# Linear attention over 32 heads on one core: stores issued from the first output on, and the written-out orders of all engines rearranged

## The chip, the core and the metric

The kernel runs on one core of a Trainium2 chip. A core has a matrix engine (PE in the profile, with its weight loads as PEld), two engines for elementwise work (VectorE, DVE; ScalarE, ACT), GpSimd (POOL), and SyncE (SP), which here only issues DMA transfers. The metric is the device time of one execution in microseconds (us), and less is better.

## The reference

Inputs q, k and v have the shape 1 x 32 x 2048 x 128 in bf16: 32 heads, 2048 rows of 128 values. Per head, with phi(x) = (x + 1 where x > 0, else exp(x)) + 1e-6:

```python
kv  = einsum("bhsd,bhse->bhde", phi_k, v)     # 128 x 128 per head, a sum over all rows
z   = einsum("bhsd->bhd", phi_k)
num = einsum("bhqd,bhde->bhqe", phi_q, kv)
den = einsum("bhqd,bhd->bhq", phi_q, z)[..., None] + 1e-6
out = num / den
```

So each head needs all of its k and v before any of its outputs, and 2 MB of q, k, v and output move per head (0.5 MB each).

## The kernel before, in words

A head's 2048 rows lie on 128 partitions as 16 tiles of 128 columns. phi(x) is taken apart into min(exp(x), 1) + 1e-6 and max(x, 0), and both parts go through the matrix engine as two matmuls into one sum. All names below are keys of the program; a key is an operation, the head, a dot and a part.

- `ldq`, `ldk`, `ldv` (L324, SP): loads of a head, 512 KB each, into buffers that hold seven heads (`NI`). `st` (L418, SP): the store of a head's output from one of twelve output buffers (`NO`); head 31 is stored in three parts.
- `ek` (L336, ACT) takes exp(k); `em` (L339, DVE) does the min and the add. `rkd` (L342, DVE) and `rkp` (L346, POOL) take max(k, 0), half of the tiles each. `v1` (L350, POOL) copies v beside a column of ones.
- `T` (L368, PE) transposes q's 16 tiles into PSUM. `eq` (L372, ACT) takes exp of it, `emq` (L374, DVE) the min and add; `rqa` (L378, ACT) and `rqb` (L381, DVE) take max(q, 0), half each.
- `kv` (L357, PE) sums the 32 matmuls of a head, in two parts of 16; `kvs` (L362, ACT) copies the 128 x 129 result out of PSUM.
- `n` (L389, L394, L396, PE) makes numerators and denominators: `n.0` for 12 tiles in four PSUM banks, `n.1` for 4 tiles in two. `r` (L403, DVE) inverts the denominators, `f` (L410, DVE) multiplies. Constants (`ident`, `ones`, `eps0` to `eps2`, `v1ones`) are set up first, and `w0` to `w2` (L315) are warm-up matmuls.

Every engine runs its operations in the order written in the table `ORDER` (lines 83 to 144), strictly, and waits on counting semaphores for the dependencies that `add` is given. There is no loop that decides anything at run time. The dependencies that matter here: `T(h)` waits until `eq`, `rqa` and `rqb` of head h-1 have read PSUM; `n(h+1).0` waits until `f(h).0` has emptied the banks; `kvs(h)` waits for both parts of `kv(h)`; `st(h)` waits for both parts of `f(h)`; a load of head h waits until head h-7 has left its buffer. SP is one queue in order, so a store that waits holds back each load behind it.

Two waits of POOL are there by choice and not for data (`gate`, called with the head from the third on):

```python
return [f"r{h - 3}.0"] if name == "v1" else [f"f{h - 3}.0"]
```

So `v1(h)` may not start before `r(h-3).0` has ended, nor `rkp(h)` before `f(h-3).0`.

Of the kernel before, what the change touches and what calls it, by code (L numbers as in the profile page):

```python
# [74 lines left out]
def rqb_parts(h):  # L75
    if na(h) == 16:
        return ()
    if h == NH - 1:
# [3 lines left out]

ORDER = {
    "PE": """
        w2 w1 T0.0 T0.1 w0 kv0.0 kv0.1 T1.0 n0.0 kv1.0 kv1.1 n0.1 T2.0 n1.0 kv2.0 kv2.1 T3.0 n1.1 kv3.0 kv3.1 n2.0
        T4.0 n2.1 kv4.0 kv4.1 n3.0 T5.0 n3.1 kv5.0 kv5.1 n4.0 T6.0 n4.1 kv6.0 kv6.1 n5.0 T7.0 n5.1 kv7.0 kv7.1 n6.0
        T8.0 n6.1 kv8.0 kv8.1 n7.0 T9.0 n7.1 kv9.0 kv9.1 n8.0 T10.0 n8.1 kv10.0 kv10.1 n9.0 T11.0 n9.1 kv11.0 kv11.1
        n10.0 T12.0 n10.1 kv12.0 kv12.1 n11.0 T13.0 n11.1 kv13.0 kv13.1 n12.0 T14.0 n12.1 kv14.0 kv14.1 n13.0 T15.0
# [5 lines left out]
        n30.0 n30.1 n31.0 n31.1 n31.2  # L94
    """,
    "DVE": """
        rkd0.0 v1ones0 em0.0 eps0 em0.1 rkd1.0 rqb0.0 ones emq0.0 eps2 emq0.1 eps1 em1.0 v1ones1 r0.0 rqb1.0 f0.0
        rkd2.0 rkd3.0 emq1.0 em2.0 em3.0 r1.0 emq2.0 rqb2.0 r0.1 f0.1 rkd4.0 f1.0 em4.0 rqb3.0 r1.1 rkd5.0 f1.1 r2.0
        emq3.0 f2.0 em5.0 rqb4.0 r2.1 rkd6.0 f2.1 r3.0 emq4.0 f3.0 em6.0 rqb5.0 r3.1 rkd7.0 f3.1 r4.0 emq5.0 f4.0
        em7.0 rqb6.0 r4.1 rkd8.0 f4.1 r5.0 emq6.0 f5.0 em8.0 rqb7.0 r5.1 rkd9.0 f5.1 r6.0 emq7.0 f6.0 em9.0 rqb8.0  # L100
        r6.1 f6.1 emq8.0 r7.0 rkd10.0 f7.0 em10.0 rqb9.0 r7.1 f7.1 emq9.0 r8.0 rkd11.0 f8.0 em11.0 r8.1 rqb10.0 f8.1
        rkd12.0 r9.0 emq10.0 f9.0 em12.0 r9.1 rqb11.0 f9.1 rkd13.0 r10.0 emq11.0 f10.0 em13.0 r10.1 rqb12.0 f10.1
        emq12.0 r11.0 rkd14.0 f11.0 em14.0 r11.1 rqb13.0 f11.1 emq13.0 r12.0 rkd15.0 f12.0 em15.0 rqb14.0 r12.1
        rkd16.0 f12.1 r13.0 emq14.0 f13.0 em16.0 r13.1 rqb15.0 f13.1 rkd17.0 r14.0 emq15.0 f14.0 em17.0 rqb16.0
        r14.1 rkd18.0 f14.1 r15.0 emq16.0 f15.0 em18.0 rqb17.0 r15.1 rkd19.0 f15.1 r16.0 emq17.0 f16.0 em19.0
        rqb18.0 r16.1 rkd20.0 f16.1 r17.0 emq18.0 f17.0 em20.0 rqb19.0 r17.1 f17.1 emq19.0 r18.0 rkd21.0 f18.0
        em21.0 r18.1 rqb20.0 f18.1 emq20.0 r19.0 rkd22.0 f19.0 em22.0 r19.1 rqb21.0 f19.1 rkd23.0 r20.0 emq21.0
        f20.0 em23.0 r20.1 rqb22.0 f20.1 emq22.0 r21.0 rkd24.0 f21.0 em24.0 rqb23.0 r21.1 f21.1 rkd25.0 r22.0
        emq23.0 f22.0 em25.0 r22.1 rqb24.0 f22.1 emq24.0 r23.0 rkd26.0 f23.0 em26.0 rqb25.0 r23.1 rkd27.0 f23.1
        r24.0 emq25.0 f24.0 em27.0 r24.1 rqb26.0 f24.1 rkd28.0 r25.0 emq26.0 f25.0 em28.0 r25.1 rqb27.0 f25.1  # L110
        rkd29.0 r26.0 emq27.0 f26.0 em29.0 rqb28.0 r26.1 rkd30.0 f26.1 r27.0 emq28.0 f27.0 em30.0 r27.1 rqb29.0
        f27.1 rkd31.0 r28.0 emq29.0 f28.0 em31.0 r28.1 rqb30.0 f28.1 r29.0 emq30.0 f29.0 emq31.2 emq31.0 r29.1 f29.1
        r30.0 f30.0 r30.1 emq31.1 f30.1 r31.0 f31.0 r31.1 r31.2 f31.1 f31.2
    """,
    "ACT": """
        eq0.0 rqa0 ek0.0 ek0.1 eq0.1 ek1.0 kvs0 eq1.0 rqa1 ek2.0 kvs1 ek3.0 eq2.0 rqa2 kvs2 ek4.0 eq3.0 kvs3 rqa3
        ek5.0 eq4.0 kvs4 rqa4 ek6.0 eq5.0 kvs5 rqa5 ek7.0 eq6.0 kvs6 rqa6 ek8.0 eq7.0 kvs7 rqa7 ek9.0 eq8.0 kvs8
        rqa8 ek10.0 eq9.0 kvs9 rqa9 ek11.0 eq10.0 kvs10 rqa10 ek12.0 eq11.0 kvs11 rqa11 ek13.0 eq12.0 kvs12 rqa12
        ek14.0 eq13.0 kvs13 rqa13 ek15.0 eq14.0 kvs14 rqa14 ek16.0 eq15.0 kvs15 rqa15 ek17.0 eq16.0 kvs16 rqa16
        ek18.0 eq17.0 kvs17 rqa17 ek19.0 eq18.0 kvs18 rqa18 ek20.0 eq19.0 kvs19 rqa19 ek21.0 eq20.0 kvs20 rqa20  # L120
        ek22.0 eq21.0 kvs21 rqa21 ek23.0 eq22.0 kvs22 rqa22 ek24.0 eq23.0 kvs23 rqa23 ek25.0 eq24.0 kvs24 rqa24
        ek26.0 eq25.0 kvs25 rqa25 ek27.0 eq26.0 kvs26 rqa26 ek28.0 eq27.0 kvs27 rqa27 ek29.0 eq28.0 kvs28 rqa28
        ek30.0 eq29.0 kvs29 rqa29 ek31.0 eq30.0 kvs30 rqa30 eq31.2 eq31.0 eq31.1 kvs31 rqa31
    """,
    "POOL": """
        ident0 ident rkp0.0 v10.0 v10.1 v11.0 rkp1.0 rkp2.0 v12.0 rkp3.0 v13.0 v14.0 rkp4.0 v15.0 rkp5.0 v16.0
# [3 lines left out]
        v128.0 rkp28.0 v129.0 rkp29.0 v130.0 rkp30.0 v131.0 rkp31.0  # L130
    """,
    "SP": """
        ldq0.0 ldk0.0 ldv0.0 ldk1.0 ldq1.0 ldv1.0 ldk2.0 ldk3.0 ldq2.0 ldv2.0 ldq3.0 ldk4.0 ldv3.0 ldv4.0 ldk5.0
        ldq4.0 ldk6.0 ldv5.0 ldq5.0 ldk7.0 ldv6.0 ldv7.0 ldq6.0 ldk8.0 ldq7.0 ldv8.0 ldk9.0 ldq8.0 ldq9.0 ldv9.0
        st0.0 ldq10.0 ldv10.0 ldk10.0 ldk11.0 ldk12.0 ldk13.0 ldv11.0 ldv12.0 ldv13.0 ldq11.0 ldq12.0 ldv14.0 st1.0
        ldk14.0 ldk15.0 ldk16.0 ldq13.0 ldk17.0 ldv15.0 ldv16.0 ldq14.0 ldq15.0 ldv17.0 ldk18.0 ldq16.0 ldq17.0
        ldq18.0 st2.0 ldq19.0 ldk19.0 ldv18.0 ldk20.0 st3.0 st4.0 ldv19.0 ldk21.0 ldq20.0 st5.0 ldq21.0 st6.0 st7.0
        ldv20.0 st8.0 ldq22.0 ldv21.0 ldv22.0 ldk22.0 ldk23.0 ldv23.0 st9.0 ldq23.0 st10.0 ldk24.0 ldk25.0 ldq24.0
        ldv24.0 ldv25.0 ldv26.0 ldq25.0 ldq26.0 st11.0 ldv27.0 ldk26.0 st12.0 ldq27.0 ldk27.0 ldq28.0 st13.0 ldv28.0
        ldk28.0 st14.0 ldq29.0 ldk29.0 ldq30.0 ldv29.0 st15.0 ldv30.0 ldk30.0 st16.0 st17.0 ldk31.0 st18.0 st19.0  # L140
        ldv31.0 ldq31.0 st20.0 st21.0 st22.0 st23.0 st24.0 st25.0 st26.0 st27.0 st28.0 st29.0 st30.0 st31.0 st31.1
        st31.2
    """,
# [320 lines left out]
```

## Time and profile before

| | |
|---|---|
| median of four runs | 170.49 us (170.21 to 171.46) |
| the profiled execution: its time, and its span from the first to the last instruction | 171.01 us, 169.6 us |
| busy over the span: PE, DVE, ACT, POOL | 158.8, 154.6, 153.7, 85.2 us |
| DMA | 67.53 MB, mean 398 GB/s |
| granted clock of PE | 0.998 of full speed |

The page of the profile gives busy time for each engine, the span in 40 slices, the DMA queues, the chain of work that ended last, and groups of instructions by line. The trace behind it has every instruction with start and duration, and for each transfer the moments of issue and landing. Because each engine runs the written order, the n-th instruction of an engine is the n-th key of its list, and so every record can be given its key; the same holds for the transfers of SP. [...] the next instruction starts about 0.1 us before the end of the one ahead.

### The profile page before, as it was taken

What the parts mean: (1) busy time and instruction counts of PE and PEld (TensorE: products, weight loads), DVE (VectorE), ACT (ScalarE), POOL (GpSimd) and SP (SyncE); (2) the same over time, 40 slices, a digit from 0 to 9 for tenths busy, and PEclk for the clock granted to TensorE, in tenths of its full rate; (3) what the DMA queues carried; (4) which work ended last, traced back from release to release, by engine and by line L of the source; (5) the groups of instructions that cost most, each with busy time, mean ns of one, the idle gap of its engine ahead of it and who ended that gap; (6) DMA issues with size and microseconds to landing.
All of it is one profiled execution on the core that took longest, in us unless ns stands there. A gap on an engine that the chain in (4) does not pass through costs nothing.

```text
span 169.6 us, 6305 instructions
## 1 busy us (share of the span) xinstructions
PE 158.8 (94%) x2775; PEld 153.6 (91%) x2775; DVE 154.6 (91%) x267; ACT 153.7 (91%) x133; POOL 85.2 (50%) x71
## 2 busy tenths in 40 slices
PE   6988789999999999999999999999999999999950
PEld 2667689999999999999999999999999999999950
DVE  0189999999999999999999999999999999999893
ACT  3699959999999999999999999999999999997810
POOL 1436444566554555555555665456554566545000
PEclk9999999999999999999999999999999999999999
DMA  5999999999999999999999999999999999999875
GB/s 203 389 418 414 406 410 408 407 410 408 414 408 410 411 413 411 406 409 415 413 420 413 412 421 414 412 415 411 416 414 420 413 414 420 413 415 415 360 318 211
DMA packets 18748, 67.53 MB, mean 398 GB/s; under 512 B 2080, under 2 KB 2464, under 8 KB 18720
## 3 DMA queue, kind: packets, MB, share of 16 engines
q1 hardware_dynamic: 18720, 67.12, 98.5%
q8 instruction: 22, 0.36, 0.8%
q14 instruction: 6, 0.05, 0.1%
HBM read 50.33 MB, written 16.78 MB: 396 GB/s over the span
## 4 chain that ended last, share of the span: by engine, by line
PE 86%; DVE 8%; ACT 3%; issue 1%; POOL 0%; POOLq 0%
PE la L357 31%; PE la L394 19%; PE la L396 17%; PE la L368 16%; DVE la L410 3%; DVE la L374 2%; PE la L315 2%; DVE la L342 1%; ACT la L372 1%; ACT la L336 1%; DVE la L381 1%; PE la L389 1%; DVE la L403 1%; ACT la L378 1%; POOL la L301 0%
## 5 line engine op out<-in xcount | busy, mean ns | idle before, releaser
L410 DVE TENSOR_TENSOR la<-la 128x1536 bf16<-128x1536 f32 (+2 forms) x65 | 77.7, 1197 | 0.3
L396 PE MATMUL la<-la 128*128 128x129 bf16 x512 | 68.1, 220 | 0.0
L394 PE MATMUL la<-la 128*128 128x129 bf16 x512 | 68.1, 219 | 0.0
L372 ACT ACTIVATE la<-la 128x2048 bf16<-128x2048 bf16 (+2 forms) x35 | 60.4, 1731 | 5.2 <-PE la L368 3.5
L357 PE MATMUL la<-la 128*128 128x129 bf16 x1024 | 64.0, 219 | 0.3 <-DVE la L305 0.3
L336 ACT ACTIVATE la<-la 128x2048 bf16<-128x2048 bf16 (+1 forms) x33 | 61.3, 1861 | 0.0
L357 PEld LDWEIGHTS la<-la 128*128 128x128 bf16 x1024 | 60.0, 97 | 0.7 <-POOL la L350 0.7
L350 POOL COPY la<-la 128x1024 int32<-128x1024 int32 (+1 forms) x33 | 39.9, 1210 | 40.8 <-DVE la L403 30.7
L346 POOL TENSOR_SCALAR la<-la 128x1024 bf16<-128x1024 bf16 x32 | 44.7, 1397 | 29.2 <-DVE la L410 25.2
L396 PEld LDWEIGHTS la<-la 128*128 128x128 bf16 x512 | 49.5, 97 | 0.0
L394 PEld LDWEIGHTS la<-la 128*128 128x128 bf16 x512 | 47.1, 97 | 0.0
L389 PE MATMUL la<-la 128*128 128x3 bf16 (+1 forms) x192 | 32.3, 168 | 4.1 <-DVE la L410 1.5
L368 PE MATMUL la<-la 128*128 128x128 bf16 x512 | 33.9, 219 | 0.4 <-DVE la L381 0.4
L378 ACT ACTIVATE la<-la 128x1024 bf16<-128x1024 bf16 (+1 forms) x32 | 33.5, 1046 | 0.0
L368 PEld LDWEIGHTS la<-la 128*128 128x128 bf16 x512 | 29.4, 98 | 1.3 <-DVE la L381 0.6
L339 DVE TENSOR_SCALAR la<-la 128x2048 bf16<-128x2048 bf16 (+1 forms) x33 | 23.0, 699 | 2.8 <-ACT la L336 2.8
L389 PEld LDWEIGHTS la<-la 128*128 128x128 bf16 x192 | 18.7, 97 | 4.9 <-DVE la L410 1.7
L374 DVE TENSOR_SCALAR la<-la 128x2048 bf16<-128x2048 bf16 (+2 forms) x35 | 22.7, 650 | 0.2
L381 DVE TENSOR_SCALAR la<-la 128x1024 bf16<-128x1024 bf16 x31 | 20.9, 674 | 0.8 <-ACT la L372 0.3
L342 DVE TENSOR_SCALAR la<-la 128x1024 bf16<-128x1024 bf16 x32 | 15.1, 475 | 5.5 <-DMA la<-in_k_dram 5.5
L403 DVE RECIPROCAL la<-la 128x12 f32<-128x12 f32 (+2 forms) x65 | 13.0, 201 | 2.7 <-PE la L396 1.0
L362 ACT ACTIVATE la<-la 128x129 bf16<-128x129 f32 x32 | 9.0, 282 | 1.9 <-PE la L357 1.9
(14 smaller groups left out, 11.7 us busy)
## 6 DMA issues: line engine op xcount, KB each, us to landing
la<-in_q_dram SPq DMA_DIRECT2D x32, 512.0 KB, 15.3
la<-in_k_dram SPq DMA_DIRECT2D x32, 512.0 KB, 14.9
la<-in_v_dram SPq DMA_DIRECT2D x32, 512.0 KB, 15.4
out_dram<-la SPq DMA_DIRECT2D x31, 512.0 KB, 15.3
out_dram<-la SPq DMA_DIRECT2D x2, 192.0 KB, 2.5
out_dram<-la SPq DMA_DIRECT2D x1, 128.0 KB, 2.7
```

Of the source, the lines that this page charges most:

```text
L336: add("ACT", f"ek{h}.{i}", lambda e, a=a, b=b: e.activation(em_sb[:, h % NE, a:b], k_sb[:, h % NI, a:b], ACT.Exp), over("ldk", h, ld_parts ...
L346: add("POOL", f"rkp{h}.{i}", lambda e, a=a, b=b: e.tensor_scalar(rk_sb[:, h % NR, a:b], k_sb[:, h % NI, a:b], BIG, 0.0, op0=ALU.min, op1=A ...
L350: add("POOL", f"v1{h}.{i}", lambda e, a=a, b=b: e.tensor_copy(v1_sb[:, h % NV, a:b, 0:D].bitcast(i32), v_sb[:, h % NI, a:b].bitcast(i32)), ...
L357: ins = e.matmul(kv_ps, lhsT=src[:, j], rhs=v1_sb[:, h % NV, j, 0:NC], start=(j + part == 0), stop=(j == NT - 1 and part == 1))
L368: ins = e.transpose(xT[:, j], q_sb[:, h % NI, j], ident[:])
L372: add("ACT", f"eq{h}.{i}", lambda e, a=a, b=b: e.activation(emq_sb[:, h % NQ, a:b], xT[:, a:b], ACT.Exp), over("T", h, t_parts, a, b) + fr ...
L374: add("DVE", f"emq{h}.{i}", lambda e, a=a, b=b: e.tensor_scalar(emq_sb[:, h % NQ, a:b], emq_sb[:, h % NQ, a:b], 1.0, EPS, op0=ALU.min, op1 ...
L378: add("ACT", f"rqa{h}", lambda e: e.activation(rq_sb[:, h % NQ, 0:n], xT[:, 0:n], ACT.Relu), over("T", h, t_parts, 0, n) + freed(NQ, h, (" ...
L389: e.matmul(_ap(o_ps[:, :], o + D, [[NC, m]]), lhsT=ones[:], rhs=epsr[:, 0:m], start=True, stop=False, skip_group_check=True)
L394: e.matmul(to, lhsT=emq_sb[:, h % NQ, t], rhs=kvs_sb[:, h % NK], start=False, stop=False, skip_group_check=True)
L396: ins = e.matmul(to, lhsT=rq_sb[:, h % NQ, t], rhs=kvs_sb[:, h % NK], start=False, stop=True, skip_group_check=True)
L410: return e.tensor_tensor(out=_ap(o_sb[:, :, :, :], first(o_sb[:, h % NO, t0, 0:1]) - first(o_sb[:, :, :, :]), [[m * D, nb], [D, m], [1, D] ...
```

## The change

Only the table `ORDER` is changed. No operation, size, buffer or dependency differs. On SP the first stores move ahead among the loads (`st0` from place 31 to place 18, `st1` from 44 to 34, and then about one store for four loads), so that the stores are spread over the loads; from `ldv31` on the list is as before. PE swaps two warm-ups and `n0.1` with `T2.0`. ACT takes both parts of `eq0` first and moves `eq31.2`. DVE's list is rearranged at the start and end and in the places of `rkd` and `rqb` among its neighbours in the middle.

```diff
 ORDER = {
     "PE": """
-        w2 w1 T0.0 T0.1 w0 kv0.0 kv0.1 T1.0 n0.0 kv1.0 kv1.1 n0.1 T2.0 n1.0 kv2.0 kv2.1 T3.0 n1.1 kv3.0 kv3.1 n2.0
+        w1 w2 T0.0 T0.1 w0 kv0.0 kv0.1 T1.0 n0.0 kv1.0 kv1.1 T2.0 n0.1 n1.0 kv2.0 kv2.1 T3.0 n1.1 kv3.0 kv3.1 n2.0
...
     "DVE": """
-        rkd0.0 v1ones0 em0.0 eps0 em0.1 rkd1.0 rqb0.0 ones emq0.0 eps2 emq0.1 eps1 em1.0 v1ones1 r0.0 rqb1.0 f0.0
-        rkd2.0 rkd3.0 emq1.0 em2.0 em3.0 r1.0 emq2.0 rqb2.0 r0.1 f0.1 rkd4.0 f1.0 em4.0 rqb3.0 r1.1 rkd5.0 f1.1 r2.0
+        eps0 rkd0.0 v1ones0 em0.0 rqb0.0 em0.1 v1ones1 eps2 emq0.0 rkd1.0 ones emq0.1 eps1 em1.0 r0.0 rqb1.0 f0.0
+        emq1.0 rkd2.0 em2.0 rkd3.0 r1.0 em3.0 rqb2.0 emq2.0 r0.1 f0.1 rkd4.0 f1.0 em4.0 rqb3.0 r1.1 rkd5.0 f1.1 r2.0
...
         r6.1 f6.1 emq8.0 r7.0 rkd10.0 f7.0 em10.0 rqb9.0 r7.1 f7.1 emq9.0 r8.0 rkd11.0 f8.0 em11.0 r8.1 rqb10.0 f8.1
-        rkd12.0 r9.0 emq10.0 f9.0 em12.0 r9.1 rqb11.0 f9.1 rkd13.0 r10.0 emq11.0 f10.0 em13.0 r10.1 rqb12.0 f10.1
-        emq12.0 r11.0 rkd14.0 f11.0 em14.0 r11.1 rqb13.0 f11.1 emq13.0 r12.0 rkd15.0 f12.0 em15.0 rqb14.0 r12.1
+        r9.0 rkd12.0 emq10.0 f9.0 em12.0 r9.1 rqb11.0 f9.1 rkd13.0 r10.0 emq11.0 f10.0 em13.0 r10.1 rqb12.0 f10.1
+        rkd14.0 r11.0 emq12.0 f11.0 em14.0 rqb13.0 r11.1 rkd15.0 f11.1 r12.0 emq13.0 f12.0 em15.0 rqb14.0 r12.1
...
-        rqb18.0 r16.1 rkd20.0 f16.1 r17.0 emq18.0 f17.0 em20.0 rqb19.0 r17.1 f17.1 emq19.0 r18.0 rkd21.0 f18.0
+        rqb18.0 r16.1 f16.1 r17.0 rkd20.0 emq18.0 f17.0 em20.0 rqb19.0 r17.1 f17.1 rkd21.0 r18.0 emq19.0 f18.0
...
-        f20.0 em23.0 r20.1 rqb22.0 f20.1 emq22.0 r21.0 rkd24.0 f21.0 em24.0 rqb23.0 r21.1 f21.1 rkd25.0 r22.0
-        emq23.0 f22.0 em25.0 r22.1 rqb24.0 f22.1 emq24.0 r23.0 rkd26.0 f23.0 em26.0 rqb25.0 r23.1 rkd27.0 f23.1
-        r24.0 emq25.0 f24.0 em27.0 r24.1 rqb26.0 f24.1 rkd28.0 r25.0 emq26.0 f25.0 em28.0 r25.1 rqb27.0 f25.1
-        rkd29.0 r26.0 emq27.0 f26.0 em29.0 rqb28.0 r26.1 rkd30.0 f26.1 r27.0 emq28.0 f27.0 em30.0 r27.1 rqb29.0
-        f27.1 rkd31.0 r28.0 emq29.0 f28.0 em31.0 r28.1 rqb30.0 f28.1 r29.0 emq30.0 f29.0 emq31.2 emq31.0 r29.1 f29.1
-        r30.0 f30.0 r30.1 emq31.1 f30.1 r31.0 f31.0 r31.1 r31.2 f31.1 f31.2
+        f20.0 em23.0 rqb22.0 r20.1 rkd24.0 f20.1 r21.0 emq22.0 f21.0 em24.0 rqb23.0 r21.1 f21.1 r22.0 rkd25.0
+        emq23.0 f22.0 em25.0 rqb24.0 r22.1 f22.1 emq24.0 r23.0 rkd26.0 f23.0 em26.0 rqb25.0 r23.1 rkd27.0 f23.1
+        r24.0 emq25.0 f24.0 em27.0 r24.1 rqb26.0 f24.1 rkd28.0 r25.0 emq26.0 f25.0 em28.0 r25.1 rqb27.0 f25.1 r26.0
+        rkd29.0 emq27.0 f26.0 em29.0 rqb28.0 r26.1 f26.1 rkd30.0 r27.0 emq28.0 f27.0 em30.0 rqb29.0 r27.1 rkd31.0
+        f27.1 r28.0 emq29.0 f28.0 em31.0 r28.1 rqb30.0 f28.1 r29.0 emq30.0 f29.0 emq31.0 emq31.1 r29.1 f29.1 r30.0
+        f30.0 r30.1 emq31.2 f30.1 r31.0 f31.0 r31.1 r31.2 f31.1 f31.2
     """,
     "ACT": """
-        eq0.0 rqa0 ek0.0 ek0.1 eq0.1 ek1.0 kvs0 eq1.0 rqa1 ek2.0 kvs1 ek3.0 eq2.0 rqa2 kvs2 ek4.0 eq3.0 kvs3 rqa3
+        eq0.0 eq0.1 ek0.0 ek0.1 rqa0 ek1.0 kvs0 eq1.0 rqa1 ek2.0 kvs1 ek3.0 eq2.0 rqa2 kvs2 ek4.0 eq3.0 kvs3 rqa3
...
-        ek30.0 eq29.0 kvs29 rqa29 ek31.0 eq30.0 kvs30 rqa30 eq31.2 eq31.0 eq31.1 kvs31 rqa31
+        ek30.0 eq29.0 kvs29 rqa29 ek31.0 eq30.0 kvs30 rqa30 eq31.0 eq31.1 kvs31 eq31.2 rqa31
...
     "SP": """
-        ldq0.0 ldk0.0 ldv0.0 ldk1.0 ldq1.0 ldv1.0 ldk2.0 ldk3.0 ldq2.0 ldv2.0 ldq3.0 ldk4.0 ldv3.0 ldv4.0 ldk5.0
-        ldq4.0 ldk6.0 ldv5.0 ldq5.0 ldk7.0 ldv6.0 ldv7.0 ldq6.0 ldk8.0 ldq7.0 ldv8.0 ldk9.0 ldq8.0 ldq9.0 ldv9.0
-        st0.0 ldq10.0 ldv10.0 ldk10.0 ldk11.0 ldk12.0 ldk13.0 ldv11.0 ldv12.0 ldv13.0 ldq11.0 ldq12.0 ldv14.0 st1.0
...
-        ldk28.0 st14.0 ldq29.0 ldk29.0 ldq30.0 ldv29.0 st15.0 ldv30.0 ldk30.0 st16.0 st17.0 ldk31.0 st18.0 st19.0
+        ldq0.0 ldk0.0 ldv0.0 ldk1.0 ldq1.0 ldv1.0 ldk2.0 ldq2.0 ldk3.0 ldv2.0 ldq3.0 ldk4.0 ldv3.0 ldv4.0 ldk5.0
+        ldq4.0 ldv5.0 st0.0 ldk6.0 ldq5.0 ldv6.0 ldv7.0 ldk7.0 ldq6.0 ldq7.0 ldq8.0 ldk8.0 ldv8.0 ldv9.0 ldk9.0
+        ldq9.0 ldk10.0 ldq10.0 st1.0 ldk11.0 ldq11.0 ldv10.0 st2.0 ldq12.0 ldv11.0 ldk12.0 ldq13.0 st3.0 ldv12.0
+        ldk13.0 ldv13.0 st4.0 ldv14.0 ldk14.0 ldv15.0 st5.0 ldq14.0 ldk15.0 ldq15.0 ldk16.0 ldk17.0 st6.0 ldv16.0
+        ldv17.0 ldk18.0 ldq16.0 ldv18.0 ldq17.0 ldq18.0 ldv19.0 st7.0 ldk19.0 ldk20.0 ldk21.0 st8.0 ldq19.0 ldk22.0
+        ldq20.0 ldv20.0 st9.0 ldq21.0 ldv21.0 ldv22.0 st10.0 ldq22.0 ldk23.0 st11.0 ldq23.0 ldk24.0 ldv23.0 st12.0
+        ldq24.0 ldk25.0 ldv24.0 st13.0 ldq25.0 ldk26.0 ldv25.0 ldv26.0 st14.0 ldq26.0 ldk27.0 st15.0 ldv27.0 ldq27.0
+        ldk28.0 st16.0 ldv28.0 ldk29.0 ldq28.0 st17.0 ldv29.0 ldq29.0 ldk30.0 ldv30.0 st18.0 ldk31.0 ldq30.0 st19.0
         ldv31.0 ldq31.0 st20.0 st21.0 st22.0 st23.0 st24.0 st25.0 st26.0 st27.0 st28.0 st29.0 st30.0 st31.0 st31.1
         st31.2
```

More of the change, by code (lines that the diff above doesn't have):

```diff
@@ L101 @@
         r6.1 f6.1 emq8.0 r7.0 rkd10.0 f7.0 em10.0 rqb9.0 r7.1 f7.1 emq9.0 r8.0 rkd11.0 f8.0 em11.0 r8.1 rqb10.0 f8.1
-        rkd12.0 r9.0 emq10.0 f9.0 em12.0 r9.1 rqb11.0 f9.1 rkd13.0 r10.0 emq11.0 f10.0 em13.0 r10.1 rqb12.0 f10.1
-        emq12.0 r11.0 rkd14.0 f11.0 em14.0 r11.1 rqb13.0 f11.1 emq13.0 r12.0 rkd15.0 f12.0 em15.0 rqb14.0 r12.1
-        rkd16.0 f12.1 r13.0 emq14.0 f13.0 em16.0 r13.1 rqb15.0 f13.1 rkd17.0 r14.0 emq15.0 f14.0 em17.0 rqb16.0
+        r9.0 rkd12.0 emq10.0 f9.0 em12.0 r9.1 rqb11.0 f9.1 rkd13.0 r10.0 emq11.0 f10.0 em13.0 r10.1 rqb12.0 f10.1
@@ L105 @@
+        rkd14.0 r11.0 emq12.0 f11.0 em14.0 rqb13.0 r11.1 rkd15.0 f11.1 r12.0 emq13.0 f12.0 em15.0 rqb14.0 r12.1
+        rkd16.0 f12.1 r13.0 emq14.0 f13.0 em16.0 rqb15.0 r13.1 rkd17.0 f13.1 r14.0 emq15.0 f14.0 em17.0 rqb16.0
         r14.1 rkd18.0 f14.1 r15.0 emq16.0 f15.0 em18.0 rqb17.0 r15.1 rkd19.0 f15.1 r16.0 emq17.0 f16.0 em19.0
-        rqb18.0 r16.1 rkd20.0 f16.1 r17.0 emq18.0 f17.0 em20.0 rqb19.0 r17.1 f17.1 emq19.0 r18.0 rkd21.0 f18.0
-        em21.0 r18.1 rqb20.0 f18.1 emq20.0 r19.0 rkd22.0 f19.0 em22.0 r19.1 rqb21.0 f19.1 rkd23.0 r20.0 emq21.0
@@ L113 @@
-        r30.0 f30.0 r30.1 emq31.1 f30.1 r31.0 f31.0 r31.1 r31.2 f31.1 f31.2
+        rqb18.0 r16.1 f16.1 r17.0 rkd20.0 emq18.0 f17.0 em20.0 rqb19.0 r17.1 f17.1 rkd21.0 r18.0 emq19.0 f18.0
+        em21.0 r18.1 rqb20.0 f18.1 rkd22.0 r19.0 emq20.0 f19.0 em22.0 r19.1 rqb21.0 f19.1 rkd23.0 r20.0 emq21.0
+        f20.0 em23.0 rqb22.0 r20.1 rkd24.0 f20.1 r21.0 emq22.0 f21.0 em24.0 rqb23.0 r21.1 f21.1 r22.0 rkd25.0
+        emq23.0 f22.0 em25.0 rqb24.0 r22.1 f22.1 emq24.0 r23.0 rkd26.0 f23.0 em26.0 rqb25.0 r23.1 rkd27.0 f23.1
@@ L132 @@
     "SP": """
-        ldq0.0 ldk0.0 ldv0.0 ldk1.0 ldq1.0 ldv1.0 ldk2.0 ldk3.0 ldq2.0 ldv2.0 ldq3.0 ldk4.0 ldv3.0 ldv4.0 ldk5.0
-        ldq4.0 ldk6.0 ldv5.0 ldq5.0 ldk7.0 ldv6.0 ldv7.0 ldq6.0 ldk8.0 ldq7.0 ldv8.0 ldk9.0 ldq8.0 ldq9.0 ldv9.0
-        st0.0 ldq10.0 ldv10.0 ldk10.0 ldk11.0 ldk12.0 ldk13.0 ldv11.0 ldv12.0 ldv13.0 ldq11.0 ldq12.0 ldv14.0 st1.0
[L136 to L139, printed above, removed]
-        ldk28.0 st14.0 ldq29.0 ldk29.0 ldq30.0 ldv29.0 st15.0 ldv30.0 ldk30.0 st16.0 st17.0 ldk31.0 st18.0 st19.0
+        ldq0.0 ldk0.0 ldv0.0 ldk1.0 ldq1.0 ldv1.0 ldk2.0 ldq2.0 ldk3.0 ldv2.0 ldq3.0 ldk4.0 ldv3.0 ldv4.0 ldk5.0
[6 more added lines that the diff above has]
+        ldk28.0 st16.0 ldv28.0 ldk29.0 ldq28.0 st17.0 ldv29.0 ldq29.0 ldk30.0 ldv30.0 st18.0 ldk31.0 ldq30.0 st19.0
         ldv31.0 ldq31.0 st20.0 st21.0 st22.0 st23.0 st24.0 st25.0 st26.0 st27.0 st28.0 st29.0 st30.0 st31.0 st31.1
```

## The prediction

> **What bounds the kernel now.** I read the page first, for who is full and where in the span.
>
> ```profile
> span 169.6 us, 6305 instructions
> PE   6988789999999999999999999999999999999950
> DVE  0189999999999999999999999999999999999893
> ACT  3699959999999999999999999999999999997810
> DMA  5999999999999999999999999999999999999875
> ```
>
> A slice is 4.24 us. PE, DVE, ACT and DMA are all full from the sixth slice on; only the first 25 us and the last 9 us have room. In the trace `kv3.0` begins at 25.12 and `kv31.0` at 157.42, so 28 heads take 132.3 us, 4.725 us each, and every single head takes that: PE sets the pace there and waits for nothing. So the middle can only be kept or spoilt, and a gain must come from the start.
>
> Second, the waits, for what PE lacks at the start:
>
> ```profile
> ACT la L362 <- PE la L357: 1.9, 1, 1.9
> PE la L389 <- DVE la L374: 1.2, 1, 1.2
> PE la L389 <- DVE la L306: 0.8, 1, 0.8
> PE la L389 <- ACT la L362: 0.6, 1, 0.6
> ```
>
> `n0.0` waited 0.8 us for the constant `eps1`, `n1.0` 1.2 us for `emq1.0`. The timeline of DVE and of POOL around that wait shows why `emq1.0` was late:
>
> ```profile
> 15.28 1.74 DVE L410 TENSOR_TENSOR la<-la 128x1536 bf16<-128x1536 f32 x1
> 16.93 2.19 DVE L342 TENSOR_SCALAR la<-la 128x1024 bf16<-128x1024 bf16 x2
> 19.05 0.68 DVE L374 TENSOR_SCALAR la<-la 128x2048 bf16<-128x2048 bf16 x1
> ...
> 16.63 1.04 POOL L350 COPY la<-la 128x1024 int32<-128x1024 int32 x1 [1.47 <-DMA la<-in_v_dram]
> 17.64 1.21 POOL L346 TENSOR_SCALAR la<-la 128x1024 bf16<-128x1024 bf16 x1
> ```
>
> Two `rkd` (L342, two instructions in one row) took 2.19 us ahead of `emq1.0` (L374), where one takes 0.42 us alone. Each ended 0.28 us after a POOL instruction ended (17.67 and 18.85): they stood still meanwhile.
>
> Third, the end. `f31.2` ends at 166.83 and the last store lands at 169.55, 2.72 us later. By the landing marks the transfers before it land 1.2 to 1.28 us apart, but for four steps of 2.2 to 2.8 that I take as they are, until `st30` at 167.64, so DMA is no more than about a microsecond behind PE as a bound.
>
> **What the Trainium skill says.** "SBUF — State Buffer", section "SBUF: two separate sides": VectorE in its two-port modes and GpSimd share a pair of ports as an exclusive lock, held for a whole instruction, and the loser "fully blocks". The trace agrees (rows above). It shows more: with one instruction waiting on each side they alternate. `rkp3` waited for `rkd2` and then went ahead of `rkd3`; `rkp1` for `emq0.1`, and ahead of `em1.0`. After the lock is won, POOL needs 0.89 us more and a full-head DVE instruction 0.55. "VectorE: DVE Perf Modes", section "Why PSUM operands drop a tier", explains why `rqb` and `f`, which read PSUM, ran beside POOL unslowed (0.69 and 1.75 us with and without): they don't use both ports.
>
> **The change, part by part.**
>
> *Start.* I rewrote the start with the new orders, the old durations and the lock. ACT: `eq0.1` ahead of `ek0` and `rqa0` behind it leaves `ek1.0` at 10.15 (was 10.17) and `kvs0` at 11.95, nothing. `eps1` is now ahead of `em1.0`, so `n0.0` starts when `kvs0` ends, 12.3 for 12.91: gain 0.6. `T2.0`, no longer behind `n0.1`, starts when `kv1` is through, 15.6 (was 17.52). `f0.0` ends at 16.45; `emq1.0` comes next, starts at 16.36, ahead of `v12`, whose data land at 16.58, and ends at 17.0. `n0.1` still waits for `kvs1` (17.0), then `n1.0` follows at 17.5 instead of 19.78. Now `rkd2`, `em2.0` and POOL's `v12`, `rkp3` alternate: 17.89, 18.17, 19.06, and `em2.0` ends at 19.6, so `kv2` starts at 19.65 (was 21.27): 1.6. `T3.0` waits for `rqa2` (21.4) and `rqb2` (21.3): 21.5 for 23.71. `emq2.0` at 21.25 is 0.4 us ahead of `v13`. `f0.1` ends at 22.65 (was 24.53), `f1.0` at 24.7. `kv3` starts after `n1.1` at 23.2 (was 25.12), `n2.0` at 25.0 (26.96), `T4.0` at 26.8 once `rqa3` is done (28.45). Gain at head 4: **1.65 us**. Loads for it: `ldq4` lands at 25.26 and `ldk5` at 23.97, in time. If either race of `emq` against `v1` (margins of 0.4 us) is lost, about 0.7 us of it goes.
>
> *Stores.* Landing by place in the queue doesn't change: 1.266 us after a load for a load, 1.281 load to store, 1.207 store to load, 1.241 store to store (means of the trace); the new mixture has four more of each turn, and sums to 0.08 us less over the whole queue. `st0` at place 18 makes SP wait for `f0.1`. The 17 loads ahead of it last until 26.5, and a transfer takes 2.4 us beyond its data time (`st31.2`: 2.7 for 128 KB), so DMA runs dry only if `f0.1` ends after 24.1; 22.65 is early enough. Cost 0; with the old 24.53 it would be 0.4. Further stores follow their `f` by 19 us or more: no wait. Loads become later against their users, since stores go ahead of them: the closest are `ldq30` with 1.1 us (was 11), `ldk30` 1.1, `ldq16` 1.4. So loads cover a shift of about 1.1 us, not more.
>
> *Middle.* In heads 9, 17, 22 and 26 `rkd` moves from ahead of `r.0` to behind it: `r rkd emq f`. DVE does the same work, but `r(h)` releases `v1(h+3)`. Head 9 before:
>
> ```profile
> 61.89 0.42 DVE L342 TENSOR_SCALAR la<-la 128x1024 bf16<-128x1024 bf16 x1
> 62.22 0.23 DVE L403 RECIPROCAL la<-la 128x12 f32<-128x12 f32 x1
> 62.36 0.63 DVE L374 TENSOR_SCALAR la<-la 128x2048 bf16<-128x2048 bf16 x1
> 62.91 1.75 DVE L410 TENSOR_TENSOR la<-la 128x1536 bf16<-128x1536 f32 x1
> ...
> 62.51 1.37 POOL L350 COPY la<-la 128x1024 int32<-128x1024 int32 x1 [1.18 <-DVE la L403]
> ```
>
> Before, `emq10` had the lock when `v112` came. Now `rkd12` has it, `v112` waits, and by the alternation goes ahead of `emq10`. `r9.0` starts 0.33 earlier, but behind it come `rkd12`, 0.89 of copy and then `emq10`: `f9.0` ends 0.85 us later (the copy less what rounding leaves), against a slack of 0.10 between `f9.0` and `n10.0`. The bounds are 0 (POOL doesn't go first) and 0.85; I take **0.75 us**, kept to the end because PE has no slack. In heads 17, 22 and 26 the copy's data land at 99.9, 123.8 and 142.8 by place. With PE 0.9 us early, `emq` is under way before that, and costs nothing.
>
> *End.* The new places of `eq31` and `emq31` move work before 160.9, where `r30.0` waits for PE; then the same chain runs from `n30.0`. 0.
>
> *Sum.* PE: -1.65 + 0.75 = -0.9, so `f31.2` ends at 165.9 and its store could land at 168.65. DMA: `st30` lands at 167.56, and `st31`'s 512 KB need 1.25 us at the queue's pace, 168.8, or 168.5 at the pace in which its parts landed before. I take 168.7 for the span of 169.55 to the last landing: -0.85. The profiled execution would go from 171.01 to 170.16; the median, which stands 0.52 lower, from 170.49 to **169.6 us**.
>
> **Rivals.**
> 1. *Races lost at the start.* `v12` or `v13` takes the lock first: -0.9 at the start, +0.75 at head 9: 170.3. For it: margins of 0.4 us; against: landings at the start are even.
> 2. *Slower: the lock is lost in all four heads.* If PE isn't at least about 0.1 us early on reaching head 17, `v120`'s data are there when `rkd20` runs, the 0.75 is paid, and then at 22 and 26 too. With a start that gains only 0.6: -0.6 + 4 x 0.75 = +2.4, 172.9; with 1.0, half that. Against: the start must miss by a microsecond. It decides from a start gain below 0.7 us.
> 3. *SP's wait at `st0` leaves DMA dry*, with `f0.1` as late as before: the DMA end moves by 0.4, to 170.05.
> 4. *No lock at head 9*: PE is 1.1 us early, where loads stop it, and DMA still ends at 168.7: 169.6 as well.
>
> **How the numbers follow.** About 0.5%, 0.85 us, is what a measurement of this kernel can tell from no change. Forecast with rival 4: 0.53 (169.2 to 170.0, somewhat over half of it beyond the bound); rivals 1 and 3: 0.24 (170.0 to 170.9); rival 2: 0.18 (171.3 to 172.9); a gain past the DMA end, by a better pace of the mixture: 0.05. Faster: 0.31 + 0.05 = 0.36. Slower: 0.18 and 0.06 of unforeseen delays within rival 1: 0.24. Same: 0.40. Range 169.0 to 171.8, which leaves out most of rival 2 and little below.
>
> **What would show it.** `n1.0` at about 17.5 and `T4.0` near 26.8; SP idle at `st0` until about 22.7 with DMA still full; an `emq10` of some 1.5 us with PE idle before `n10.0`, and no such at 17, 22, 26; heads of 4.725 us elsewhere; `f31.2` near 165.9 with DMA full beyond it. Wrong if PE shows waits for loads after head 10, if more than one `emq` is stretched, or if `T4.0` is later than 28.

## The result, and the profile after

The changed kernel is slower: 171.41 us median of 35 runs (170.09 to 172.60) against 170.87 us of 54 runs of the kernel before (170.02 to 171.46). The ratio is **1.0036, with a 95% interval of 1.0024 to 1.0048**. Its runs spread over 2.5 us, those of before over 1.4. A ratio, here and below, leaves out runs more than 1.5% above the fastest of the same kernel, which matters in experiment 7 alone. The profiled execution took 170.84 us, the fourth fastest of the 35. Its span is 169.4 us, where the median span of the 35 runs is 170.1 and the profile of before has 169.6. So this page shows where PE and DMA gained and lost time, but not the loss of the median run; for that the experiments are needed.

The page of the changed kernel, its head and the rows in 40 slices:

```profile
span 169.4 us, 6304 instructions
PE   6988989999999999999999999999999999999950
DVE  0187999999999999999999999999999999999892
ACT  3799999999999999999999999999999999996800
DMA  5999999999999999999999999999999999999985
```

At this grain little differs but the start: ACT's sixth slice, half empty before (5), is full. There the forecast held closely. The timeline of DVE in the changed kernel (start, duration, operation) has `f0.0`, `emq1.0`, `rkd2.0`, `em2.0` in the new order, with `emq1.0` at 16.36 and no wait for the lock:

```profile
14.70 1.75 DVE L410 TENSOR_TENSOR la<-la 128x1536 bf16<-128x1536 f32 x1
16.36 0.68 DVE L374 TENSOR_SCALAR la<-la 128x2048 bf16<-128x2048 bf16 x1
16.96 0.42 DVE L342 TENSOR_SCALAR la<-la 128x1024 bf16<-128x1024 bf16 x1
17.30 0.69 DVE L339 TENSOR_SCALAR la<-la 128x2048 bf16<-128x2048 bf16 x1
```

`n1.0` starts at 17.51, `kv3.0` at 23.22, `f0.1` ends at 22.64, `T4.0` starts at 26.55 (28.45 before): PE is **1.90 us early** from head 3 on. At the end it is 0.69 us early (`f31.2` 166.14, before 166.83). The last store still lands at 169.40, 3.26 us after `f31.2`, because `st30` landed at 168.07, later than before (167.64). So two things need a cause: 1.2 us of PE's lead is lost on the way, and DMA, which now sets the end, isn't earlier than before but 0.4 us later.

**Where PE's lead goes.** The waits of POOL for v, first of the kernel before, then of the changed one (total, times, longest):

```profile
POOL la L350 <- DMA la<-in_v_dram: 9.2, 5, 2.7
```

```profile
POOL la L350 <- DMA la<-in_v_dram: 27.2, 13, 3.1
```

Ten of the thirteen are copies from head 10 on that start when their data land, after their gate; in the kernel before only `v131` does. What that does is seen in the timeline of the changed kernel around head 8, DVE and then POOL:

```profile
51.46 1.75 DVE L410 TENSOR_TENSOR la<-la 128x1536 bf16<-128x1536 f32 x1
53.12 1.38 DVE L339 TENSOR_SCALAR la<-la 128x2048 bf16<-128x2048 bf16 x1
...
52.92 1.04 POOL L350 COPY la<-la 128x1024 int32<-128x1024 int32 x1 [3.08 <-DMA la<-in_v_dram]
```

The gate would have placed `v110` under `f7.0` (51.46 to 53.21), which reads PSUM. Its data came at 52.80, so it took the port pair 0.2 us ahead of `em10.0` (L339), which then took 1.38 us where 0.68 is usual. PE's lead falls there from 1.91 to 1.38. `em23`, `em24` and `em25` (0.93, 0.95, 0.99 us) take 0.7 more together, for the same reason. No `emq` is stretched, at head 9 either: the data of `v112` landed at 61.57, when `emq10` (60.79 to 61.48) was through.

**Where DMA's time goes.** SP has issued 17 loads by 10.7 us and then waits for `f0.1` until 22.67. The windows of the profile show what DMA does then. Each row has the stretch, its length, the busy time of PE, PEld, DVE, ACT and POOL, the clock, the busy share of DMA and its GB/s. The kernel before, and then the changed one:

```profile
23.00:26.00 3.00, 2.56 (x47) 2.38 (x45) 2.97 (x6) 2.70 (x3) 1.04 (x1) 1.00 1.03 408
26.00:29.00 3.00, 3.00 (x58) 2.99 (x56) 2.83 (x7) 3.00 (x4) 1.41 (x1) 1.00 1.02 407
```

```profile
23.00:26.00 3.00, 3.00 (x59) 3.00 (x57) 2.87 (x4) 2.97 (x4) 2.16 (x2) 1.00 1.00 377
26.00:29.00 3.00, 3.00 (x58) 2.99 (x56) 3.00 (x7) 3.00 (x3) 1.54 (x2) 1.00 0.99 392
```

(408 - 377) x 3 + (407 - 392) x 3 = 138 KB that DMA did not move, 0.34 us at its pace, in an execution in which `f0.1` was as early as forecast. A second profile of the changed kernel misses 183 KB.

### The profile page after: what moved, and what is told of

Read it like the earlier page. It is cut to its first block, busy times and chain, and to the rows that moved or that the text cites. A ratio compares the mean times of both kernels' runs of the same rounds, so it can differ in the third digit from the quotient of the medians.

```text
span 169.4 us, 6304 instructions
## 1 busy us (share of the span) xinstructions
PE 159.3 (94%) x2775; PEld 153.4 (91%) x2775; DVE 154.1 (91%) x267; ACT 154.3 (91%) x133; POOL 84.4 (50%) x71
## 4 chain that ended last, share of the span: by engine, by line
DVE 40%; ACT 30%; PE 24%; issue 3%; POOL 0%; DVEq 0%; POOLq 0%
DVE la L410 19%; ACT la L372 14%; ACT la L336 10%; PE la L357 8%; DVE la L381 6%; PE la L394 5%; ACT la L378 5%; DVE la L374 5%; PE la L368 5%; PE la L396 5%; DVE la L339 4%; DVE la L342 3%; DVE la L403 2%; PE la L315 2%; ACT la L362 1%
## 5 line engine op out<-in xcount | busy, mean ns | idle before, releaser
L339 DVE TENSOR_SCALAR la<-la 128x2048 bf16<-128x2048 bf16 (+1 forms) x33 | 24.5, 742 | 2.9 <-ACT la L336 2.9
L374 DVE TENSOR_SCALAR la<-la 128x2048 bf16<-128x2048 bf16 (+2 forms) x35 | 21.1, 603 | 0.0
```

The costliest lines, as they stand in the source:

```text
L339: add("DVE", f"em{h}.{i}", lambda e, a=a, b=b: e.tensor_scalar(em_sb[:, h % NE, a:b], em_sb[:, h % NE, a:b], 1.0, EPS, op0=ALU.min, op1=AL ...
```

## The experiments

Each ran beside the kernel before on the same chip, with a ratio to it. The three kinds of change (start, stores, middle of DVE) are taken apart first, then `st0` alone. The diffs of experiments 1, 3 and 10 are against the kernel before, those of 2, 5 and 7 against the changed one; "..." is what is left out of a long list. Two theories stand in the expectations from the start: A, late loads put `v1` on `em`; B, DMA is slower by itself when stores are mixed in early.

**1. The stores alone.**

```diff
     "SP": """
-        ... ldq4.0 ldk6.0 ldv5.0 ldq5.0 ...
+        ... ldq4.0 ldv5.0 st0.0 ldk6.0 ldq5.0 ...
```

> The kernel before with SP's new order alone (stores early), PE, DVE, ACT as before. Theory A (late loads: v1 copies that wait for their data fall on em, the port pair is taken, PE loses up to 0.5 us each time, and PE's head start of 1.9 us is what makes loads late): PE has no head start here, v1 is at most 0.1 us late at its gate, no em is stretched; ratio 0.999 to 1.001, at most 0.3 us for SP's wait at st0 (f0.1 ends at 24.5 here). Theory B (DMA itself is slower with stores mixed in from the start): the loss is all here, ratio 1.003 to 1.005, and the landing of st30 in the trace moves later by 0.5 us or more.

Measured 1.0068 (1.0042 to 1.0095), 172.40 us. Theory A missed, and B seemed nearer, with more than its 1.005; neither named the cause. `f0.1` ends at 24.6 here, and DMA moves 251 GB/s from 23 to 26 us and 328 from 26 to 29: 708 KB missing. `ldq31` lands at 156.00 (before 153.86), and late copies stretch `em20` and `em31` to 1.38 and 1.36 us.

**2. The engines alone**: the changed kernel with SP as before.

```diff
     "SP": """
-        ... ldq4.0 ldv5.0 st0.0 ldk6.0 ldq5.0 ...
+        ... ldq4.0 ldk6.0 ldv5.0 ldq5.0 ...
```

> The kernel after with SP's order of before: loads early, all other orders new. Theory A: PE is 1.9 us early at head 4 and no v1 is late for its data; but where rkd stands between r.0 and emq (heads 9, 17, 22, 26) the copy v1 is there and takes the port pair between the two, 0.75 us each; with two to four of these PE keeps 0 to 0.4 us: ratio 0.998 to 1.006. If the copy doesn't go ahead, PE keeps about 1.1 us and DMA's end bounds the kernel: ratio 0.995. Theory B: DMA as in the kernel before, ratio 0.995 to 1.000.

Measured 1.0086 (1.0058 to 1.0114), 172.82 us, the worst of the parts. The timeline of DVE and POOL at head 9 has the prediction's lock: `r9.0`, `rkd12`, `emq10`, `f9.0`, and `v112`:

```profile
60.73 0.22 DVE L403 RECIPROCAL la<-la 128x12 f32<-128x12 f32 x1
60.87 0.36 DVE L342 TENSOR_SCALAR la<-la 128x1024 bf16<-128x1024 bf16 x1
61.15 1.52 DVE L374 TENSOR_SCALAR la<-la 128x2048 bf16<-128x2048 bf16 x1
62.59 1.74 DVE L410 TENSOR_TENSOR la<-la 128x1536 bf16<-128x1536 f32 x1
...
61.01 1.11 POOL L350 COPY la<-la 128x1024 int32<-128x1024 int32 x1 [0.84 <-DVE la L403]
```

`emq10`, `emq18`, `emq23` and `emq27` each take 1.52 us for 0.63; PE loses 0.80, 0.74, 0.75 and 0.79 there and goes from 1.16 early to 1.89 late. With loads in time each of the four places costs what I had priced for one.

**3. The start alone**: the first lines of PE, DVE and ACT new (DVE's two as in the change), all else as before.

```diff
     "PE": """
-        w2 w1 T0.0 T0.1 ... kv1.1 n0.1 T2.0 n1.0 ...
+        w1 w2 T0.0 T0.1 ... kv1.1 T2.0 n0.1 n1.0 ...
     "ACT": """
-        eq0.0 rqa0 ek0.0 ek0.1 eq0.1 ek1.0 ...
+        eq0.0 eq0.1 ek0.0 ek0.1 rqa0 ek1.0 ...
```

> The kernel before with only the first lines of the orders of PE, DVE and ACT new (to head 5), stores and middle as before. Both theories: PE is 1.9 us early at head 4, no stretched em in the middle, loads stop PE at ldk28 to ldk30 so that about 1.1 us is kept; DMA ends at about 168.7 in the trace; ratio 0.994 to 0.997, a version faster than both. If the ratio is 0.999 or more, PE's lead is worth nothing because DMA alone sets the end.

Measured **0.9977** (0.9963 to 0.9991), 170.41 us: faster than both kernels. The size missed. PE is only 0.66 us early in this profile: `em2` and `emq2` lost the lock to `rkp3` and `v13` (1.53 and 1.56 us), the lost race of my first rival. Over all ten profiles with the new start PE's lead at head 4 is 0.66 to 2.04 us. No load stopped it.

**4. The changed kernel again.**

> The changed kernel once more, for a second profile and a ratio on the same chip: 1.0036 by its first measurement. Theory A: in a profile with a span near 170.1 more em instructions are stretched than the four of the first profile (em10, em23, em24, em25), and f31.2 ends near 167 or later. Theory B: f31.2 near 166.2 again and the landing of st30 later than 168.1.

Measured 1.0030 (1.0011 to 1.0050). The profiled span is 169.4 again, so what was expected of a longer one was not tried. Behind the start four `em` are stretched (`em10`, `em20`, `em25`, `em31`), and `f31.2` ends at 166.32.

**5. Start and stores, the middle of DVE as before.** One of the places in the list:

```diff
     "DVE": """
-        r9.0 rkd12.0 emq10.0 f9.0 ...
+        rkd12.0 r9.0 emq10.0 f9.0 ...
```

> The first lines of PE, DVE and ACT new and SP's order new, the middle of DVE as before: the changed kernel without its four heads of r, rkd, emq. Theory A (late loads put v1 on em): as the changed kernel, em10 and two to four of em20 to em31 stretched to 0.9 to 1.4 us, ratio 1.000 to 1.004, against 0.9977 of the same kernel with the stores as before. Theory B (the mixture of stores and loads makes DMA itself slower): the same ratio, but no difference in it from stretched em; st30 lands after 168.1. A third, that the new middle of DVE is the loss: 0.998.

Measured 1.0040 (1.0016 to 1.0064). As A has it, six `em` are stretched (0.79 to 1.16 us), and as B has it, `st30` lands at 168.62: the two are not told apart. It rules out the third: the middle of DVE isn't needed for the loss.

**6. The same with the loads sorted by due time**, stores in their places.

> As start_and_stores, each store at the same place, but the loads between them (from place 19 to 114) sorted by when they are due, a v by its gate. By place v25, v24, v23, v20 and v10, which were late by 0.7 to 1.8 us for a PE that is 1.9 us early, come in time; v28, v29 and v30 stay 0.9 to 1.9 us late. Theory A: no em stretched before em28, PE ends about as in start_only (f31.2 near 166.2), ratio 0.996 to 0.999. Theory B: no better than start_and_stores, 1.000 to 1.004.

Measured 1.0039 (1.0025 to 1.0053), no better, though no `em` before `em29` is stretched in the profile. So A, as stated, fell. (My sorting had its own price: `T29` waited 1.1 us for `ldq29`. But `st30` lands at 169.17, so DMA sets the end here too.) What experiments 1, 5 and 6 share is `st0` at place 18.

**7. `st0` alone moved later in the changed kernel.**

```diff
-        ldq4.0 ldv5.0 st0.0 ldk6.0 ldq5.0 ldv6.0 ldv7.0 ldk7.0 ldq6.0 ldq7.0 ...
+        ldq4.0 ldv5.0 ldk6.0 ldq5.0 ldv6.0 ldv7.0 ldk7.0 ldq6.0 st0.0 ldq7.0 ...
```

> The changed kernel with st0 alone moved from place 18 to 24. If part of the loss is the dip of DMA at 25.25 us behind SP's wait for f0.1, DMA gains up to 0.3 us and ldk6 to ldq6 land 1.25 us earlier: ratio 1.000 to 1.002. If st0 has no part in it: 1.003 to 1.004 as for the changed kernel.

Fourteen runs lie between 169.66 and 173.34 us, median 172.10: five below 170.6, seven above 172.3. The ratio of 0.9985 (0.9956 to 1.0014) covers only half of them and is not used; the median is no better than the changed kernel's. The profiled execution is one of the longer ones (172.69 us). In it DMA is full at 24 us, loads are in time (`ldq31` at 153.18), and so all four `emq` are 1.52 us long, as in experiment 2. That the runs below 170.6 miss the lock is argued, not shown.

**8. `rkd` put back ahead of `r` in the four heads**, alone and with `st0` later. Theory C joins two effects: SP's wait at `st0` costs DMA time and makes all loads late; where loads are in time instead, the lock in the four heads costs.

> The changed kernel with rkd12, rkd20, rkd25 and rkd29 put back ahead of r9.0, r17.0, r22.0 and r26.0; all else new. Theory C (a switch: where loads come in time, v1 goes between rkd and emq in four heads, 0.75 us each, as engines_only and st0_later showed; where they come late, v1 falls on em instead): the first half of the switch is gone. No emq of 1.5 us in the profile, the times above 172 us become rare, ratio 0.998 to 1.002 with a narrower spread than 170.1 to 172.8. If the loss has nothing to do with these four places: 1.003 to 1.004, as start_and_stores (1.004) would have it.

> As rkd_back, and st0 moved from place 18 to 24. Theory C with the cost of st0 (10 or more of the 16 DMA engines run dry about 2.5 us before the landing mark, so that an f0.1 later than 22.9 us costs DMA time and makes all loads late): both halves are gone; no emq and at most one em stretched, ldq31 lands before 153.5, PE keeps 0.6 to 1.9 us, DMA sets the end; ratio 0.995 to 0.998. If stores among the loads are the loss by themselves: 1.002 or more.

Measured 1.0051 (1.0032 to 1.0070) alone, so that expectation missed: with `st0` early the lock in the middle isn't what costs, and no `emq` of the middle is stretched in the profile. With `st0` later: **0.9956** (0.9940 to 0.9971), 169.97 us. One key moved by six places is 1.6 us between the medians. The windows of the two, `rkd_back` and then with `st0` later:

```profile
23.00:26.00 3.00, 2.36 (x43) 2.37 (x44) 3.00 (x4) 2.62 (x2) 0.97 (x2) 1.00 0.87 339
26.00:29.00 3.00, 3.00 (x60) 2.99 (x58) 2.87 (x8) 3.00 (x4) 1.87 (x2) 1.00 0.97 336
```

```profile
23.00:26.00 3.00, 2.22 (x41) 2.16 (x40) 2.97 (x5) 2.72 (x2) 0.97 (x2) 1.00 1.02 406
26.00:29.00 3.00, 3.00 (x60) 2.99 (x58) 2.87 (x8) 3.00 (x4) 1.87 (x2) 1.00 1.03 411
```

At head 4 PE is 0.96 us early in the first and 0.76 in the second, and `f0.1` ends at 23.6 and 23.8. In the first DMA misses 420 KB, 1.0 us; in the second nothing. `ldq31` lands at 155.56 and 153.49, and where loads are late four `em` of the middle are stretched again (one in the other).

**9. DMA by itself.**

> All arithmetic is left out (outputs are a constant): only the 130 transfers in SP's order of before, a load waiting for the earlier load of its buffer, a store for the fill of its buffer. Measures DMA's own time for this order: about 2 us to the first data, 128 transfers of 1.25 us and a few stalls, so a span of 166 to 168.5.

> The same for SP's new order. Theory B (the mixture of loads and stores is slower for DMA itself): at least 0.5 us longer than dma_only_before. Theory C: within 0.2 us of it, since the order of the transfers alone costs nothing.

Measured 167.34 and 167.10 us (medians of six). The page of each, order of before and new order:

```profile
span 165.8 us, 164 instructions
DMA packets 18721, 67.13 MB, mean 405 GB/s; under 512 B 2080, under 2 KB 2464, under 8 KB 18720
```

```profile
span 165.5 us, 164 instructions
DMA packets 18721, 67.13 MB, mean 406 GB/s; under 512 B 2080, under 2 KB 2464, under 8 KB 18720
```

Theory B fell: the order of the transfers costs nothing when nothing waits. One thing stays open here. In the order of before the last landing comes at 165.84, 3.7 us earlier than in the whole kernel (169.55). The page of the kernel before lists a queue that the pages of these two runs lack (packets, MB, share of the 16 engines):

```profile
q8 instruction: 22, 0.36, 0.8%
```

By that share each of its packets takes about 1 us of one engine. Whether they make the difference was not tried.

**10. `st0` early in the kernel before, and late among the new stores.**

```diff
-        ldq4.0 ldk6.0 ldv5.0 ldq5.0 ... ldv9.0 st0.0 ldq10.0 ...
+        ldq4.0 ldk6.0 st0.0 ldv5.0 ldq5.0 ... ldv9.0 ldq10.0 ...
```

> The kernel before with st0 alone moved from place 31 to 18, nothing else. Theory C (SP's wait at st0 empties DMA, and what is lost there is never made up): f0.1 ends at about 24.5, DMA runs mostly dry for about 1.2 us around 24 to 25.5, every later landing is that much later, last landing 170.2 or more; ratio 1.003 to 1.006. If the stores that follow early (st1 and on) are the loss: 0.999 to 1.001.

> The kernel before with SP's new order, and in it st0 at place 24 and not 18. Theory C: the 0.68% of stores_only is gone, 0.998 to 1.002; DMA stays full at 24 us, PE as before. If early stores cost by themselves: 1.003 or more.

`st0` early and nothing else: **1.0069** (1.0037 to 1.0101). The stores of experiment 1 with `st0` at place 24: 0.9993 (0.9971 to 1.0014). In `st0_early_only` SP's own rows show the wait from 10.2 to 24.5 (a load at L323, then `st0` at L417; its file is one line shorter):

```profile
9.73 0.43 SPq L323 DMA_DIRECT2D la<-in_k_dram  x1
24.53 0.35 SPq L417 DMA_DIRECT2D out_dram<-la  x1
```

DMA's row in slices of 0.25 us, from 20 to 30 us, shows what follows; first the kernel before:

```profile
DMA  9999999999999999999999999999999999999999
```

```profile
DMA  9897999989898999833106999995955999899998
```

The windows of `st0_early_only`, to be compared with those of the kernel before:

```profile
23.00:26.00 3.00, 2.58 (x48) 2.40 (x45) 2.37 (x4) 2.72 (x3) 1.16 (x2) 1.00 0.69 272
26.00:29.00 3.00, 3.00 (x58) 2.99 (x56) 2.84 (x7) 3.00 (x4) 1.41 (x1) 1.00 1.02 322
```

DMA misses 663 KB in two parts. From 24.25 to 25.25 most engines are idle, and 408 KB are missing by 26 us. In the second dip, 255 KB, the busy share is as before (1.02): the engines are not idle, but packets take up to 0.95 us where 0.16 is usual. Why they do isn't shown. PE is untouched: at every head it stands at most 0.04 us from before, and `f31.2` ends at 166.79 (166.83). But `st30` lands at 169.44 for 167.64, and the last store at 170.69 for 169.55. So the whole loss is DMA's.

Over all profiles the loss goes with the end of `f0.1` where `st0` has place 18. KB is what DMA moved less than in the kernel before from 23 to 29 us, from windows as above:

| profile | `f0.1` ends | KB missing |
|---|---|---|
| the changed kernel, again | 22.50 | 183 |
| the changed kernel | 22.64 | 138 |
| experiment 6 | 23.14 | 330 |
| experiment 5 | 23.41 | 360 |
| `rkd_back` | 23.58 | 420 |
| `st0_early_only` | 24.51 | 663 |
| experiment 1 | 24.63 | 708 |

In the six other kernels, with `st0` at place 24 or 31 and `f0.1` at 23.16 to 24.38, it is at most 12 KB.

**11. The best of it**: start and stores new, the middle of DVE as before, `st0` at place 24.

> start_and_stores (1.004) with st0 at place 24. Theory C: 0.994 to 0.998, as rkd_back_st0_later (0.9956); against 1.003 or more if something else in this order of stores is the loss. Beside start_only (0.9977) it tells whether spreading the stores is worth anything by itself.

Measured **0.9954** (0.9939 to 0.9968), 169.90 us, faster than both kernels. By the medians it is 0.5 us faster than the start alone (0.9977), but the intervals of the two ratios touch and they ran on different chips; with the old start the same stores gave 0.9993. So that spreading the stores gains by itself is likely, not shown. In the profile `em31` is still 1.16 us long and PE keeps only 0.50 us; DMA sets the end, `st30` at 168.10, last landing 169.35.

## Why the prediction was wrong

The forecast was 169.6 us, 0.85 less than before; the median measured was 171.41 against 170.87, 0.54 more.

**The step that failed is the one on stores: "DMA runs dry only if `f0.1` ends after 24.1; 22.65 is early enough. Cost 0; with the old 24.53 it would be 0.4."** Its first half, `f0.1` at 22.65, was right to 0.01 us in the first profile. The threshold was wrong. I counted from landing marks, "The 17 loads ahead of it last until 26.5". A transfer has sixteen marks in the trace, and its landing is the last. In `st0_early_only` those of place 17 run from 24.40 to 26.72. Sixteen packets are in flight until 23.9, seven at 24.25, one at 25.2, and `st0`'s own first packets start at 25.38, 0.85 us after its issue (24.53). So the engines begin to run dry unless `f0.1` ends by about 24.0 - 0.9 = 23.1, an estimate from this one profile; I had left out the time from issue to first packet and taken one moment for all engines.

Even that is too late a limit: at 22.64 and 22.50 the changed kernel misses 138 and 183 KB. The table of experiment 10 rises by about 0.27 MB per us of `f0.1`, which would reach nothing at about 22.0, an estimate beyond what was measured. Then the price: the old `f0.1` costs 663 KB, 1.6 us at DMA's pace and 1.2 us in the time (1.0069), not 0.4. Moved six places later, `st0` takes 1.0051 to 0.9956, 1.0040 to 0.9954 and 1.0068 to 0.9993 in three kernels.

With 22.65 the first profile loses little (0.34 us). But the races at the start, my first rival, decide this as well: in `rkd_back` and `start_and_stores`, whose start is the changed kernel's, `f0.1` ended at 23.6 and 23.4, and 1.0 and 0.9 us of DMA went. I had kept rivals 1 and 3 apart. They are one: a lost race delays `f0.1`, and SP turns that into lost DMA time. What spreads the changed kernel's runs over 2.5 us stays open: these two kernels, with the same start and the same `st0`, spread over 1.45 and 1.44 us in 16 and 8 runs, so the new places of `rkd` may have a part in it, and no profile of one of its longer runs was had.

**That "loads cover a shift of about 1.1 us"** was mis-sized for v. I measured v's slack against `kv`, some 4 us, and took a late copy to cost nothing. But it runs beside `f`, where it harms least, only at its gate. From head 10 on, eight copies came 1.3 us or more after their gate in the two profiles of the changed kernel. Each of them met `em`, at up to 0.6 us of PE's time; those late by less stretched none. In the first profile that took 1.2 of 1.9 us.

**The lock at head 9** was right in mechanism and size (0.75 forecast; 0.80, 0.74, 0.75, 0.79 measured in `engines_only`) but wrong in when it comes: in both profiles of the changed kernel the data of v come too late for it at all four heads. It paid at all four where loads were in time, also in heads 17, 22 and 26, where I had forecast none. So the changed kernel has two ways to lose: loads in time meet the lock behind `rkd`, late ones meet `em`. That is why `st0` later alone did not mend it (experiment 7), and why it did together with `rkd` ahead of `r` (experiment 8).

**The start** held in the two profiles of the changed kernel: forecast 1.65, measured 1.90 and 2.04. In the first, part of it was luck: the data of `v12` landed at 17.74 and not at 16.58, so `em2.0` had no lock to wait for and ended at 17.99, not at 19.6. In the eight other profiles with this start the lead is 0.66 to 1.38 us, so rival 1 is nearer to what usually happens. Luck too is that `f31.2` ended at 166.14, close to the forecast 165.9: the 0.75 at head 9 was not paid, and 1.2 us went to `em` instead.

**The DMA end as a bound**: the last landing was forecast at 168.7, and is at 169.3 to 169.5 in every profile of a kernel that kept its DMA full and PE early; `st30`, taken at the 167.64 of one execution, landed at 168.10 and 168.28 in the kernels of 0.9954 and 0.9956. But those two were profiled in the longest of their 22 runs each. Their median spans are 168.6 and 168.7 us, as the bound has it, and their gain of 0.45% is about the 0.5% forecast.

**Smaller readings.** In the page before, PE, DVE, ACT and DMA are all full from the seventh slice on, not the sixth (PE 8, ACT 5 there). The 19 us by which further stores follow their `f` don't hold for their issue: SP issued `st1` 4.5 us after `f1.1`, still without a wait. In rival 2 a start gain of 1.0 gives -1.0 + 4 x 0.75 = +2.0, not half of 2.4; `engines_only`, with 1.16, ended 1.89 late. None of the signs that the prediction named for being wrong came in the first profile: it watched PE, and the loss was DMA's.

**The rival of the other side** was the wrong one for the changed kernel: four locks at once. Of what came true, rivals 1 and 3, the second was listed at 0.4 us, and most of their chance was put under "same".

## What to carry to other kernels

A store in an in-order DMA queue is a wait for everything behind it: count when the first of the DMA engines runs out of work, not when the last transfer lands, take off the time from issue to first packet (0.85 us here), and put the store a few places later than that. When DMA has little to spare in the whole kernel, what it loses to one early wait can come out at the end, whatever the other engines do: here 663 KB missing at 24 to 29 us moved the last landing by 1.1 us. Before a queue is filled tighter, ask for each transfer not only whether its user can wait, but what that user will run beside when it is late.

## What the runs showed of the hardware that was not expected

- The sixteen marks of one transfer drift apart. Those of place 17 span 2.3 us in the kernel before (24.19 to 26.52) and 1.0 us with DMA by itself in the same order; those of place 120 span 5.4 and 1.6 us.
- The same 130 transfers take 167.34 us with the stores late and 167.10 with them spread, so their mixture is free here.
- The same orders at the start, the first 17 loads included, give PE a lead of 0.76 to 2.04 us at head 4 in eight profiles. Stretched `em` and `emq` show that races for the port pair differ between them; how much of the lead each race takes was not worked out.
- After an early wait DMA can be busy and yet slow: from 26 to 29 us in `st0_early_only` its share was 1.02 and it moved 322 GB/s, where the kernel before moved 407.
